# Block 0 of an adaLN transformer block on one core: keys due by chunk, the projection bank lent to row scores, modulation products and q/k parts on GpSimd, three pieces a projection

## The chip, the core and the metric

The kernel runs on one core of a Trainium2 chip. The core has five engines with instruction streams of their own: TensorE (PE, matrix multiplication into PSUM; its weight loads are shown as PEld), VectorE (DVE), ScalarE (ACT), GpSimd (POOL) and SyncE (SP), which here issues the DMAs. Each engine works through its stream in order; semaphores tie the streams together. The metric is the device time of one execution in microseconds, as the median over runs.

## The reference

One transformer block with adaptive layer norm: 2048 positions, width 576, 32 heads of 18, a feed-forward part of width 4608, all in float32.

```python
def _A_ref(x, wqkv, wo):                       # S = 2048, D = 576, H = 32
    qkv = (x @ wqkv).reshape(B, S, 3, H, D // H).transpose(2, 0, 3, 1, 4)
    q, k, v = qkv[0], qkv[1], qkv[2]
    p = softmax(einsum("bhqd,bhkd->bhqk", q, k) * Dh ** -0.5)
    return einsum("bhqk,bhkd->bhqd", p, v).transpose(0, 2, 1, 3).reshape(B, S, D) @ wo

def _B_ref(x, w1, w2):
    return silu(x @ w1) @ w2                   # F = 4608

mod = (silu(c) @ w_mod)                        # six vectors of 576: sa, ca, ga, sb, cb, gb
h = layernorm(x) * (1 + ca) + sa
x = x + ga * _A_ref(h, wqkv, wo)
h = layernorm(x) * (1 + cb) + sb
x = x + gb * _B_ref(h, w1, w2)
```

## The kernel before

**Precision.** Projections and feed-forward split each operand into a high part in the matmul type `float32r` and a low part (the rest), and add three products: high by high, high by low, low by high. So a q/k projection of 128 columns over 512 positions is 14 matmuls into one PSUM bank (list `PASS`), and its result is stored as a high and a low part (`qkhl`). The scores contract over three copies of the 18 head rows (54 rows), which is the same sum of products.

**Stages.** `first_part` normalizes x, transposes it to `hTh`/`hTl`, and computes v, the first two column tiles of k and, for the first 1024 positions, of q, and the first 80 row scores. Then the main loop goes over four blocks of 512 query positions (block 0 to 3) with eight quads of four heads each. Beside block 0 run the q/k projections still missing: 24 of them, `steps` and `add_qk`. Beside blocks 1 to 3 runs the output projection and feed-forward part (`post`) of the block before; that of block 3 runs alone at the end.

**A slot.** The loop counts slots; one `now` is half a slot: a matmul `psa` (line 802) of 128 queries by 512 keys, whose row maximum DVE takes (line 804), for a quad that is 40 slots ahead, and a matmul `psb` (line 852) of 128 keys by 512 queries of the current quad, whose exponential ACT takes (line 854, the tile `pt`). They use opposite row halves of PE, 64 rows each, and so run as a pair. A value step (line 889, `psv`) multiplies four `pt` tiles by v on four column strips of the array. A projection (line 591, `psqk`) uses all 128 rows. PSUM has eight banks; in block 0 three go to `psa` (pool `psA`), three to `psb`, one to the values, one to projections (`psF`).

**What sets the order.** PE's order is written out by the program itself: at each turn the main loop chooses between a score pair ("s"), value steps ("v") and the next item of a list of filler work ("f"). It does so by a clock of its own, `plan.t`, to which `plan.work` adds constants (ns): `TS` a score pair, `TV` a value step, `MMC` and `MMH` a matmul of 512 or 288 columns, `TX` for a change of the array's shape. DVE and ACT are two queues with durations (`plan.op`), and banks are rings: `plan.when("a")` says when the next bank of `psa` is free. The filler `Filler` is a list of small items, paced over the slots left; a projection stands in it as pieces of `GQ`. `fill.until` empties it up to a named item at once. The order on the other engines is not written by hand: the framework's scheduler places their instructions by a reckoning of its own.

**What block 0 fetches.** `load_quad` fetches a quad's q into SBUF and first asks with `need` for the projections of which that quad's k and q consist; `load_k` fetches a chunk of 512 keys. All go through SyncE's queue.

**The modulation products.** Of the six vectors of `mod`, two are computed in `first_part`; the other four come in block 0, 20 products in all (`cols`): `col_load` fetches a weight tile `wcl` of 128 by 576, and `col_dot` multiplies it by silu(c) (`sbc`) and sums the row, in one DVE instruction with an accumulator (line 514). The tile comes from the same ring of three buffers as `qkhl`.

**A projection's end.** The last piece of `qk_one` copies the bank twice on ACT, once as the high part (line 602) and once whole (`qt`, line 595); GpSimd subtracts (line 596); two DMAs store (lines 616 and 618).

## Time and profile before

| | |
|---|---|
| median of 3 runs | 2412.84 us (2409.73 to 2415.67) |
| profiled execution | 2407.57 us, span 2405.8 us |
| mean granted clock of PE | 0.992 |
| PE, DVE, ACT, POOL busy, of the span | 97%, 74%, 62%, 26% |
| first `psb` matmul of the main loop | 154.4 us |
| last projection matmul of block 0 | 530.4 us |
| first matmul of block 0's output projection | 577.1 us |
| last `psb` matmul | 2112.1 us |

The span is that of the profiled execution from its first to its last instruction. Engine rows give busy time; the time of an instruction on PE overlaps that of the next one, so starts tell more than busy shares there. A value matmul and a `psm` matmul are two records each in the trace, so a value step of four matmuls is eight records. In the groups, "idle before" is the engine's idle time ahead of the group's instructions, with what ended most of it.

### The profile page before, as it was taken

How to read it: one execution, taken by the hardware profiler on the slowest of the kernel's cores; microseconds unless marked ns; L12 is line 12 of the kernel's file. 1: busy time of each engine (PE TensorE's matmuls, PEld its weight loads, DVE VectorE, ACT ScalarE, POOL GpSimd, SP SyncE). 2: the span in 40 equal slices, each digit the busy share in tenths (PEclk: the TensorE clock that was granted, in tenths of full speed). 3: DMA queues.
4: the chain of work that ended last, by engine and by line, in shares of the span. 5: the costliest groups of instructions: out<-in, count | busy, mean ns of one | idle time of the engine just before them, and what ended most of it. 6: DMA issues, size and time to landing. Idle time of an engine off the chain costs nothing.

```text
span 2405.8 us, 52151 instructions
## 1 busy us (share of the span) xinstructions
PE 2323.4 (97%) x19844; PEld 1596.2 (66%) x19844; DVE 1775.2 (74%) x3109; ACT 1482.1 (62%) x2734; POOL 637.5 (26%) x769
## 2 busy tenths in 40 slices
PE   6999999998999999998999999999999999989999
PEld 4874444434567766775676777766677777678998
DVE  8768989887878888886887888887877787144333
ACT  5247777775667776675776777775676677722121
POOL 5201011104746676663311111122211111110000
PEclk9999999999999999999999999999999999999999
DMA  7555556445556666665655445554545554336563
GB/s 254 163 173 173 168 170 182 150 159 157 195 191 206 213 223 208 221 220 180 216 172 175 164 164 191 170 181 139 188 160 167 189 166 163 120 113 225 203 206 118
DMA packets 201474, 433.02 MB, mean 180 GB/s; under 512 B 31362, under 2 KB 67618, under 8 KB 201226
## 3 DMA queue, kind: packets, MB, share of 16 engines
q1 hardware_dynamic: 201226, 429.68, 54.5%
q8 instruction: 159, 2.61, 0.5%
q14 instruction: 89, 0.73, 0.1%
HBM read 338.54 MB, written 86.33 MB: 177 GB/s over the span
## 4 chain that ended last, share of the span: by engine, by line
PE 84%; DVE 7%; DMA 4%; ACT 3%; POOL 2%; issue 1%; SPq 0%; ACTq 0%; POOLq 0%; DVEq 0%
PE ps L486 25%; PE psv L889 18%; PE psa L802 13%; PE ps L480 10%; PE psb L852 8%; PE psqk L591 3%; DVE mx L804 3%; PE psp L486 2%; PE psv L486 2%; DMA raw<-in_w 1%; ACT pt L854 1%; PE psqk L486 1%; PE psv L1350 1%; PE psqk L1350 1%; PE psp L480 1%
## 5 line engine op out<-in xcount | busy, mean ns | idle before, releaser
L804 DVE TENSOR_REDUCE mx<-psa 128x1 f32<-128x512 f32 x2048 | 1319.0, 683 | 310.9 <-PE psb L852 161.8
L854 ACT ACTIVATE pt<-psb 128x512 f32<-128x512 f32 x2048 | 1131.5, 598 | 503.1 <-PE psb L852 305.8
L852 PE MATMUL psb<-qt,kb 56*128 56x512 f32 x2048 | 750.1, 423 | 10.7 <-ACT pt L854 9.7
L802 PE MATMUL psa<-ka,qt 54*128 54x512 f32 x2016 | 698.2, 415 | 9.5 <-DVE mx L804 8.0
L802 PEld LDWEIGHTS psa<-ka,qt 54*128 54x128 f32 x2016 | 335.2, 186 | 298.7 <-DVE mx L804 202.0
L889 PE MATMUL psv<-pt,vt 128*32 128x512 f32 x4096 | 513.5, 604 | 2.3 <-ACT ov L893 1.7
L486 PE MATMUL ps<-w2t,g 64*128 64x288 f32 x4992 | 410.5, 294 | 7.7 <-POOL w2t L693 3.9
L486 PEld LDWEIGHTS ps<-w2t,g 64*128 64x128 f32 x4992 | 382.7, 186 | 43.0 <-DVE mx L804 10.1
L852 PEld LDWEIGHTS psb<-qt,kb 56*128 56x128 f32 x2048 | 352.4, 185 | 53.6 <-ACT pt L854 38.4
L486 PE MATMUL ps<-hh,w1t 64*128 64x512 f32 x1944 | 371.6, 395 | 6.8 <-POOL w1t L696 3.1
L486 PEld LDWEIGHTS ps<-hh,w1t 64*128 64x128 f32 x1944 | 220.3, 186 | 44.9 <-DVE mx L804 7.5
L889 PEld LDWEIGHTS psv<-pt,vt 128*32 128x32 f32 x4096 | 99.5, 109 | 215.8 <-issue 208.0
L1125 POOL TENSOR_TENSOR g<-etmp,g 128x512 fp32r<-128x512 f32 x108 | 137.8, 1297 | 392.3 <-ACT g L1124 334.6
L1003 POOL TENSOR_TENSOR x<-x,gt 128x288 f32<-128x288 f32 x116 | 93.6, 807 | 416.9 <-ACT gt L1002 416.9
L486 PE MATMUL ps<-hl,w1t 64*128 64x512 f32 x864 | 198.0, 393 | 0.5 <-POOL hl L413 0.5
L999 DVE TENSOR_TENSOR x<-ps,x 128x288 f32<-128x288 f32 x184 | 83.8, 456 | 124.8 <-PE ps L480 77.1
L480 PE MATMUL ps<-w2t,g 128*128 128x288 f32 x960 | 133.5, 299 | 7.4 <-ACT g L1124 5.9
L480 PEld LDWEIGHTS ps<-w2t,g 128*128 128x128 f32 x960 | 131.1, 191 | 9.9 <-ACT g L1124 6.3
L486 PEld LDWEIGHTS ps<-hl,w1t 64*128 64x128 f32 x864 | 105.3, 186 | 10.8 <-POOL hl L413 0.9
L1121 ACT ACTIVATE eq<-ps 128x512 f32<-128x512 f32 x36 | 21.6, 600 | 146.3 <-PE ps L480 146.3
L480 PE MATMUL ps<-hh,w1t 128*128 128x512 f32 x360 | 106.9, 390 | 0.5 <-DVE hh L415 0.5
L1122 DVE SCALAR_TENSOR_TENSOR etmp<-etmp 128x512 f32<-128x512 f32 x108 | 76.6, 744 | 23.4 <-ACT etmp L1121 23.2
(146 smaller groups left out, 2084.4 us busy)
## 6 DMA issues: line engine op xcount, KB each, us to landing
w1t<-w1s SPq DMA_DIRECT2D x108, 640.0 KB
w2t<-w2s SPq DMA_DIRECT2D x108, 576.0 KB
kb<-kscr SPq DMA_DIRECT2D x512, 108.0 KB
ka<-kscr SPq DMA_DIRECT2D x504, 108.0 KB
w1s<-w1t SPq DMA_DIRECT2D x36, 640.0 KB
w2s<-w2t SPq DMA_DIRECT2D x36, 576.0 KB
vt<-vscr SPq DMA_DIRECT2D x32, 608.0 KB
qt<-qscr SPq DMA_DIRECT2D x128, 108.0 KB
```

Of the source, the lines that this page charges most:

```text
L480: mm(self.ps[late], lhsT=lhsT, rhs=rhs, start=(i == 0), stop=(i == self.n - 1))
L486: done = mm(self.ps[g], lhsT=lhsT[rows], rhs=rhs[rows], start=(s == 0), stop=(s == self.end))
L591: mm(qk_ps[0], lhsT=w[b][:, kt, :], rhs=(hTl if a else hTh)[:, kt, n * 512:(n + 1) * 512], start=(i == 0), stop=(i == 13))
L802: mm(ps, lhsT=t["q"][64 * j:64 * j + 54, hp, stt * P:(stt + 1) * P], rhs=t["a" if ("a", kc, hp) in t else "b", kc, hp][64 * j:64 * j + 54, ...
L804: return lambda: nc.vector.tensor_reduce(t["mx"][:, 2 * j + hp, stt, kc:kc + 1], ps, axis=AX.X, op=ALU.max)
L852: state["pe"] = mm(ps, lhsT=t["b", kt // 4, hp][64 * e:64 * e + 56, kt % 4 * P:(kt % 4 + 1) * P], rhs=t["q"][64 * e:64 * e + 56, hp, :], s ...
L854: nc.scalar.activation(t["P"][kt, hp][:, e, :], ps, AF.Exp, scale=SCALE)
L889: mm(t["ps"][32 * h:32 * h + 32, :], lhsT=t["v"][:, c0:c0 + 32], rhs=t["P"][kt, h // 2][:, h % 2, :], start=(kt == 0), stop=(kt == NKT - 1 ...
L999: nc.vector.tensor_add(c["x1"][j][:, hs], ps, c["x1"][j][:, hs])
L1003: nc.gpsimd.tensor_add(c["x1"][j][:, hs], c["x1"][j][:, hs], t)
L1122: nc.vector.scalar_tensor_tensor(t, t, 1.0, u, op0=ALU.add, op1=ALU.mult)
L1125: (nc.vector if last else nc.gpsimd).tensor_tensor(g[:, 1, :], t, f(g[:, 0, :]), op=ALU.subtract)
```

## The change

Seven edits, all but the constants in block 0:

1. A projection is cut in three pieces of 5, 5 and 4 matmuls, not in four of 4, 4, 3 and 3.
2. The planner's constants: `MMC`, `MMH`, `TS` and `TV` are lower, `TX` is higher, and a change to the full array costs two `TX`, not one. These hold in all blocks.
3. `col_dot` runs on GpSimd: a multiplication of 576 elements, then three halving additions (288, 144, 72); DVE sums the 72 left.
4. At a projection's end ACT copies the bank once; GpSimd makes the high part from that copy, then the low part. The bank is released after one ACT copy.
5. Each pair of column tiles computes q before k.
6. A quad's keys are asked for chunk by chunk, ahead of the load of each chunk, no longer all four with the quad.
7. If no bank of `psa` is free by the plan, a row score may take the projection bank when it is free.

```diff
--- before.py
+++ after.py
@@ -64,13 +64,13 @@
 GS = 2
 GR = [[range(i, min(i + GS, n)) for i in range(0, n, GS)] for n in (28, 27)]
 NG = len(GR[0])
-GQ = (range(0, 4), range(4, 8), range(8, 11), range(11, 14))
+GQ = (range(0, 5), range(5, 10), range(10, 14))
 G2 = [range(i, i + 3) for i in range(0, 24, 3)]
 GP = [range(i, i + 2) for i in range(0, 28, 2)]
-MMC = 231
-MMH = 133
-
-TS, TV, TX, TL, TR = 231, 906, 95, 430, 60
+MMC = 228
+MMH = 131
+
+TS, TV, TX, TL, TR = 229, 862, 112, 430, 60
 TMAX, TEXP = 605, 495
 TLAT = {"A": 100, "V": 85}
 AHEAD = 12
@@ -112,7 +112,7 @@
     def work(self, cost, mode="half"):
 
         if mode != self.mode:
-            cost += 2 * TX if mode == "half" else TX
+            cost += 2 * TX if mode in ("half", "full") else TX
             self.mode = mode
         self.t += cost
 
@@ -529,8 +529,16 @@
 
     def col_dot(m, t):
         w = col.pop((m, t))
-        after_pe(mod_dot(2 + m, t, w) if m < 2 else dot(w, gcol[:, m - 2, t:t + 1]))
-        plan.op("V", plan.t, 830)
+        dst = modc[:, 2 + m, t:t + 1] if m < 2 else gcol[:, m - 2, t:t + 1]
+        after_pe(nc.gpsimd.tensor_tensor(w, w, sbc, op=ALU.mult))
+        n = D
+        while n > 72:
+            n //= 2
+            nc.gpsimd.tensor_tensor(w[:, :n], w[:, :n], w[:, n:2 * n], op=ALU.add)
+        nc.vector.tensor_reduce(dst, w[:, :n], axis=AX.X, op=ALU.add)
+        if m == 1:
+            nc.vector.tensor_scalar_add(dst, dst, 1.0)
+        plan.op("V", plan.t + 6000, 160 if m == 1 else 80)
 
     def mod_load(m, t):
         dg = wqp.tile([P, P], F32, tag="dg", name="dg", bufs=1)
@@ -591,11 +599,12 @@
             mm(qk_ps[0], lhsT=w[b][:, kt, :], rhs=(hTl if a else hTh)[:, kt, n * 512:(n + 1) * 512], start=(i == 0), stop=(i == 13))
         if part == len(GQ) - 1:
 
-            hl, tmp = qk_hi(qk_ps[0]), qk_ps["t"].tile([P, 512], F32, name="qt")
+            hl, tmp = wqp.tile([P, 2, 512], F32R, tag="qk", name="qkhl", bufs=QKB), qk_ps["t"].tile([P, 512], F32, name="qt")
             nc.scalar.activation(tmp, qk_ps[0], AF.Copy)
+            nc.gpsimd.tensor_copy(hl[:, 0], tmp)
             nc.gpsimd.tensor_tensor(hl[:, 1], tmp, f(hl)[:, 0], op=ALU.subtract)
             qk_store(which, m, n, hl, (0, 1))
-            chain([("A", 600), ("A", 600)], plan.t + 200, None, qk_ps[1])
+            chain([("A", 600)], plan.t + 200, None, qk_ps[1])
 
     def qk_hi(ps):
         hl = wqp.tile([P, 2, 512], F32R, tag="qk", name="qkhl", bufs=QKB)
@@ -725,7 +734,7 @@
 
     steps = []
     for m in range(2, 4):
-        steps += [(KM, m, ((0, 1), (2, 3))), (QM, m, ((0, 1),))]
+        steps += [(QM, m, ((0, 1),)), (KM, m, ((0, 1), (2, 3)))]
     steps += [(XM, 0, ((0, 1), (2, 3)))]
     for m in range(4):
         steps += [(QM, m, ((2, 3),))]
@@ -748,9 +757,6 @@
     def load_quad(i):
         b, qd = divmod(i, NQUAD)
         t = quads.setdefault(i, {})
-        if b == 0:
-            for h in range(4 * qd, 4 * qd + 4):
-                need("k", h, 3)
         if b < NQB:
             for h in range(4 * qd, 4 * qd + 4):
                 need("q", h, b)
@@ -787,18 +793,22 @@
             load_quad(i + 1)
         n, w = divmod(s, 8)
         if w == 1:
+            i_, kc = divmod(n + 2, NKEY)
+            if i_ < NQUAD:
+                for h in range(4 * i_, 4 * i_ + 4):
+                    need("k", h, kc)
             if s == LEAD + 1:
                 load_k("a", n + 1, 0)
             load_k("a", n + 1, 1)
         elif w == 5:
             load_k("a", n + 2, 0)
 
-    def slot_mm(s, j):
+    def slot_mm(s, j, borrow=False):
         i, w = divmod(s, 32)
         kc, w = divmod(w, 8)
         hp, stt = divmod(w, 4)
         t = quads[i]
-        ps = psA.tile([P, 512], F32, tag="a", name="psa")
+        ps = psF.tile([P, 512], F32, tag="f", name="psa") if borrow else psA.tile([P, 512], F32, tag="a", name="psa")
         mm(ps, lhsT=t["q"][64 * j:64 * j + 54, hp, stt * P:(stt + 1) * P],
            rhs=t["a" if ("a", kc, hp) in t else "b", kc, hp][64 * j:64 * j + 54, :], start=True, stop=True)
         return lambda: nc.vector.tensor_reduce(t["mx"][:, 2 * j + hp, stt, kc:kc + 1], ps, axis=AX.X, op=ALU.max)
@@ -807,8 +817,9 @@
         if j == 0:
             slot_load(s)
         t = quads[s // 32]
-        slot_mm(s, j)()
-        plan.op("V", plan.t + TL - TS, TMAX, plan.take("a"))
+        borrow = not plan.is_ready(plan.when("a"))
+        slot_mm(s, j, borrow)()
+        plan.op("V", plan.t + TL - TS, TMAX, plan.take("f" if borrow else "a"))
         if j == 1 and s % 32 == 31:
             now = 2 * s + 1
             later.append((now, 0, 0, lambda: (max_a(t), max_rows(t)), None))
@@ -1554,6 +1565,9 @@
             fn()
             plan.advance()
 
+    def may_borrow():
+        return "p" not in mp and plan.is_ready(plan.when("f"))
+
     now = 2 * LEAD
     fill.pace(now, NQUAD * 64 - END0)
     stood = 0
@@ -1569,7 +1583,7 @@
         more = now < 2 * (total + LEAD)
         n = kts_ready()
         room = state["p"] + (now % 2 == 0) <= len(pts)
-        scores = more and room and plan.is_ready(plan.when("b")) and (now // 2 >= total or plan.is_ready(plan.when("a")))
+        scores = more and room and plan.is_ready(plan.when("b")) and (now // 2 >= total or plan.is_ready(plan.when("a")) or may_borrow())
         work = fill.pos < len(fill.items)
         target = fill.target() if work else now + AHEAD - 1
         ahead = now - target
```

PE, block 0, a stretch in the middle. Before, a piece of a projection (`psqk`), a run of three score pairs (`psa` and `psb` in turn) and a value step (`psv`):

```order
L591 MATMUL psqk<-hTl,wqh 128x512
L591 MATMUL psqk<-hTh,wqh 128x512
L591 MATMUL psqk<-hTh,wql 128x512
L802 MATMUL psa<-ka_82,qt 128x512
L852 MATMUL psb<-qt,kb_85 128x512
L802 MATMUL psa<-ka_82,qt 128x512
L852 MATMUL psb<-qt,kb_85 128x512
L802 MATMUL psa<-ka_83,qt 128x512
L852 MATMUL psb<-qt,kb_84 128x512
L889 MATMUL psv_3922<-pt_2036,vt_2040 32x512 x2
L889 MATMUL psv_3922<-pt_2037,vt_2040 32x512 x2
```

With the change, the last piece of a projection, a run of three pairs, a value step, and the first pair of the next run, which has three again (lines 599, 812, 863 and 900 of the change are 591, 802, 852 and 889 of before):

```order
L599 MATMUL psqk<-hTh,wql 128x512
L599 MATMUL psqk<-hTl,wqh 128x512
L599 MATMUL psqk<-hTh,wqh 128x512
L599 MATMUL psqk<-hTh,wql 128x512
L812 MATMUL psa<-ka_83,qt 128x512
L863 MATMUL psb<-qt,kb_85 128x512
L812 MATMUL psa<-ka_83,qt 128x512
L863 MATMUL psb<-qt,kb_85 128x512
L812 MATMUL psa<-ka_83,qt 128x512
L863 MATMUL psb<-qt,kb_84 128x512
L900 MATMUL psv_3981<-pt_2038,vt_2040 32x512 x2
L900 MATMUL psv_3981<-pt_2030,vt_2040 32x512 x2
```

The pieces are longer, and two pairs in a run have mostly become three. Over the whole stage from the first `psb` to the last `psqk` both orders have the same 473 score pairs, 117 value steps and 336 projection matmuls. Runs of score pairs: 194 before, 173 now; runs of full-array matmuls: 90 before, 68 now; runs of value steps: 117 in both. Sequences of three pairs, one value step and three pairs: none before, 41 now. All that stands ahead of the first `psb`, on each engine, is the same in both.

GpSimd, at the start of block 0's projections. Before, the subtraction at a projection's end (`qkhl`) and that of the next weights (`wql`):

```order
L596 TENSOR_TENSOR qkhl<-qt,qkhl 128x512 x3
L564 TENSOR_TENSOR wql<-raw,wqh 128x640
L596 TENSOR_TENSOR qkhl<-qt,qkhl 128x512 x2
L564 TENSOR_TENSOR wql<-raw,wqh 128x640
L596 TENSOR_TENSOR qkhl<-qt,qkhl 128x512 x4
L564 TENSOR_TENSOR wql<-raw,wqh 128x640
```

With the change, casts and subtractions (lines 604, 605) with the products of one modulation tile (`wcl`) among them:

```order
L604 CAST qkhl<-qt 128x512
L533 TENSOR_TENSOR wcl<-wcl,sbc 128x576
L605 TENSOR_TENSOR qkhl<-qt,qkhl 128x512
L537 TENSOR_TENSOR wcl<-wcl 128x288
L537 TENSOR_TENSOR wcl<-wcl 128x144
L537 TENSOR_TENSOR wcl<-wcl 128x72
L604 CAST qkhl<-qt 128x512
```

One instruction per projection has become two, and four more stand there per modulation tile, here with the first of them between the two of a projection.

DVE, at the first modulation product. Before, the product itself stands among the row maxima (`mx`):

```order
L804 TENSOR_REDUCE mx<-psa 128x1 x38
L514 SCALAR_TENSOR_TENSOR wcl,gcol<-wcl,sbc 128x576
L537 TENSOR_SCALAR dg<-ident,gcol 128x128
L804 TENSOR_REDUCE mx<-psa 128x1 x20
L514 SCALAR_TENSOR_TENSOR wcl,gcol<-wcl,sbc 128x576
L804 TENSOR_REDUCE mx<-psa 128x1 x7
```

With the change, the reduction of what GpSimd leaves:

```order
L814 TENSOR_REDUCE mx<-psa 128x1 x45
L538 TENSOR_REDUCE gcol<-wcl 128x1
L545 TENSOR_SCALAR dg<-ident,gcol 128x128
L814 TENSOR_REDUCE mx<-psa 128x1 x19
L829 TENSOR_REDUCE negm<-mx 128x16
L832 CAST ms<-negm 128x2x8
```

The product has left DVE's stream, the short reduction stands some rows later in it. The bank of projections is lent to one of the 472 row scores in this stage in the built program.

## The prediction

> **What bounds the kernel now.** I read the page first (busy shares, the chain that ended last), then busy time by stage, then the stage of the change one PE instruction at a time.
>
> ```profile
> span 2405.8 us, 52151 instructions
> PE 2323.4 (97%) x19844; PEld 1596.2 (66%) x19844; DVE 1775.2 (74%) x3109; ACT 1482.1 (62%) x2734; POOL 637.5 (26%) x769
> PE 84%; DVE 7%; DMA 4%; ACT 3%; POOL 2%; issue 1%; SPq 0%; ACTq 0%; POOLq 0%; DVEq 0%
> ```
>
> PE carries 84% of the chain, DVE 7%. The change sits in block 0, from the first `psb` matmul to the last projection matmul:
>
> ```profile
> L852 PE MATMUL psb<-qt,kb x2048: 386/397/625, 154.4 to 2112.1; 56*128 56x512 f32 x187
> L591 PE MATMUL psqk<-hTh,wql x120: 387/396/504, 155.6 to 530.4; 128*128 128x512 f32 x120
> 154.40:530.40 376.00, 371.65 (x2241) 157.46 (x2238) 329.84 (x584) 281.10 (x545) 40.39 (x32) 1.00 0.53 165
> 530.40:577.00 46.60, 42.91 (x238) 16.53 (x239) 38.41 (x67) 34.45 (x64) 24.15 (x34) 1.00 0.69 210
> 1200.00:1600.00 400.00, 399.54 (x3972) 289.79 (x3969) 324.38 (x542) 285.48 (x526) 65.23 (x63) 1.00 0.51 170
> ```
>
> In those 376.0 us (columns: PE, weight loads, DVE, ACT, POOL) PE is called busy for 371.65, DVE for 329.84, POOL for 40.39. Yet PE starts only 2241 instructions, 6.0 per us, against 9.9 from 1200 to 1600. So the busy share hides something, and the starts show what:
>
> ```profile
> 300.52 0.49 PE L802 MATMUL psa<-ka,qt 54*128 54x512 f32 x1
> ...
> 301.43 0.50 PE L591 MATMUL psqk<-hTl,wqh 128*128 128x512 f32 x1
> ...
> 305.72 1.06 PE L889 MATMUL psv<-pt,vt 128*32 128x512 f32 x8
> 306.72 0.49 PE L802 MATMUL psa<-ka,qt 54*128 54x512 f32 x1
> ...
> 307.38 0.50 PE L591 MATMUL psqk<-hTh,wqh 128*128 128x512 f32 x1
> 307.71 0.39 PE L591 MATMUL psqk<-hTh,wql 128*128 128x512 f32 x1
> ...
> 309.10 0.39 PE L591 MATMUL psqk<-hTh,wql 128*128 128x512 f32 x1
> 309.42 0.50 PE L802 MATMUL psa<-ka,qt 54*128 54x512 f32 x1
> 799.62 1.86 PE psv L889 x16
> 721.19 2.71 PE psv L889 x24
> ```
>
> PE runs in three shapes of the array: score pairs on row halves (`psa`, `psb`), projections on all of it (`psqk`), value steps on column strips (`psv`). Inside a run of projections starts follow by (309.10 - 307.71) / 6 = 0.23 us. The run of eight takes 309.42 - 307.38 = 2.04 = 8 x 0.23 + 0.20. The run of three pairs takes 0.91, that of two 0.66: 0.23 a pair and about 0.21 for the run. A value step (eight records) takes 1.00, two in the chain 1.86, three 2.71: 0.86 a step and 0.14 a run. So **each change of shape costs 0.14 to 0.21 us**, and a sum of steps and runs can be held against the stage:
>
> ```profile
> L852 PE MATMUL psb<-qt,kb 56*128 56x512 f32 x473 | 168.6, 442 | 2.3 <-ACT pt L854 1.7
> L889 PE MATMUL psv<-pt,vt 128*32 128x512 f32 x936 | 124.7, 604 | 0.6 <-DMA vt<-vscr 0.6
> ```
>
> 473 pairs x 0.23 = 108.8; 936 / 8 = 117 value steps x 0.857 = 100.3; 24 projections of 14 x 0.23 = 77.3; ten small `psm` about 1. Work: 287.4. The built order of before has 194 score runs, 90 projection runs and 117 value runs here: 40.7 + 18.0 + 16.4 = 75.1. Together 362.5 of 376.0: **PE waits for only some 13.5 us**, and loses 75 to changes of shape.
>
> **The change part by part.** *Runs.* With three pieces a projection and with the new planner costs, the order of the change has, for the same instructions in this stage, 173 score runs, 68 projection runs and 117 value runs. That is 21 x 0.21 + 22 x 0.20 = **8.8 us less**, directly on the path. Behind the last projection the order is the same up to the output projection of block 0. From there on only the planner's constants act: 224 score runs become 218, 219 value runs 213, 6 full-array runs 7: 1.3 + 0.8 - 0.2 = **1.9 us less**.
>
> *Products on GpSimd.* The costs:
>
> ```profile
> L804 DVE TENSOR_REDUCE mx<-psa 128x1 f32<-128x512 f32 x468 | 295.9, 682 | 45.0 <-PE psb L852 32.7 <-PE psa L802 10.4
> L514 DVE SCALAR_TENSOR_TENSOR wcl<-wcl,sbc 128x576 f32<-128x576 f32 x20 | 15.4, 769 | 0.0
> L514 DVE DVE_READ_ACCUMULATOR wcl<-wcl,sbc 128x1 f32 x20 | 1.6, 81 | 0.0
> L818 DVE TENSOR_REDUCE negm<-mx 128x16 f32<-128x64 f32 x7 | 1.5, 213 | 0.1
> L596 POOL TENSOR_TENSOR qkhl<-qt,qkhl 128x512 fp32r<-128x512 f32 x23 | 29.7, 1290 | 214.8 <-ACT qt L595 92.9 <-DVE mx L804 64.3 <-DMA kb<-kscr 29.3
> L1003 POOL TENSOR_TENSOR x<-x,gt 128x288 f32<-128x288 f32 x116 | 93.6, 807 | 416.9 <-ACT gt L1002 416.9
> L602 ACT ACTIVATE qkhl<-psqk 128x512 fp32r<-128x512 f32 x24 | 14.5, 606 | 3.6 <-PE psqk L591 3.5
> L693 POOL CAST wo<-raw x10: 417/426/466, 545.3 to 570.4; 128x288 fp32r<-128x288 f32 x10
> ```
>
> DVE loses 15.4 + 1.6 = 17.0 us and gains 20 reduces of 72 elements; the nearest row is the one of 64 elements, 0.21 us, so 4.2. Net 12.8 us free of 329.84. GpSimd gains per product 576 elements (1290 x 576 / 512 = 1.45 us), 288 (0.81), 144 and 72 (0.41 and 0.20 in proportion): 2.9 us, 20 times 58. *q/k parts.* ACT loses 24 x 0.606 = 14.5 us; GpSimd gains 24 casts of 0.426 x 512 / 288 = 0.76 each, 18. POOL goes from 40.4 to about 117 of 367 us, so it has room, and a part comes 0.76 us later to its store.
>
> None of this is PE's own work; it can take from the 13.5 us of waits, or add. The earlier release of the projection bank (one ACT copy, not two) helps in the same way. Bounds: all of them gone, -13.5; for the upper end see the rivals. I take 0, since two things pull against each other. For less waiting: DVE and ACT are 13 and 14 us freer. For more: in 41 places three pairs, one value step and three pairs now follow directly, which before has nowhere in this stage. Such a cycle is 0.21 + 0.69 + 1.00 = 1.90 us of PE, and three row maxes take
>
> ```profile
> 304.51 1.89 DVE L804 TENSOR_REDUCE mx<-psa 128x1 f32<-128x512 f32 x3 [0.37 <-PE psa L802]
> 542.19 2.48 DVE L804 TENSOR_REDUCE mx<-psa 128x1 f32<-128x512 f32 x4 [0.65 <-PE psb L852]
> 541.65 0.50 PE L802 MATMUL psa<-ka,qt 54*128 54x512 f32 x1
> ...
> 544.79 0.50 PE L802 MATMUL psa<-ka,qt 54*128 54x512 f32 x1
> ```
>
> 1.89, or 3 x 0.62 by the run of four. There is no margin, so DVE's other work in these 78 us becomes wait. That other work is 329.84 less 473 maxes at 0.63 (295.9 / 468), 31 us, less 17.0 and with 4.2: 18 us over the stage, of which 78 / 367 is 4 us. Against that stand some 4 us of the relief.
>
> *Keys by chunk.* It moves when K is due, and adds no instruction. What it removes is small:
>
> ```profile
> SPq L761 <- DMA qscr<-qkhl: 4.6, 2, 3.9
> SPq L618 <- POOL qkhl L596: 8.4, 12, 1.4
> ```
>
> Twice the queue of loads stands up to 3.9 us for a q part just stored, and key loads are queued behind it. In the new order the shortest way from a store to its load is several score runs long. Keys are fetched eight slots (sixteen scores) ahead, so I count nothing; if that cover is gone, 4.6 us. *The lent bank.* In the built program it serves 1 of the stage's row scores: nothing.
>
> Sum: -8.8 - 1.9 + 0 = **-10.7 us**: span 2395.1, that run 2396.9 for 2407.57. The median shown, 2412.84, lies 5.3 above the profiled run, so 2402.
>
> **The rivals.** *A, the waits take it back.* Each of the 41 tight cycles waits longer than its share. The row from 541.65 to 544.79 is such a case: 3.14 us for 0.21 + 0.92 + 1.00 = 2.13 of work, 1.0 lost a cycle; 41 of them would be 41 us. Against that full price: there PE stood for exponentials with two `psb` banks, and this stage has three. At 0.15 to 0.35 each, 6 to 14 us: 2408 to 2416, no change by measure.
>
> *B, slower: the reduce stands in DVE's queue.* DVE runs in order, so a reduce whose GpSimd chain isn't done holds all row maxes behind it, and these hold the score banks. The chain takes 2.9 us, 4.2 where a q/k subtraction stands inside it. For it: the SyncE row above, where the planned order trusted GpSimd too early in 12 places, by up to 1.4 us. Three banks cover about one max, 0.6; at 1.4 late 20 x 0.8 = 16 us, at 2.0 late 28. From about 1.1 us late on average it decides: 2402 + 16 to 28, 2418 to 2430. Against it: DVE's order is not written by hand; the scheduler puts the reduce where, by its own reckoning, the chain is done.
>
> ```profile
> L911 DVE TENSOR_TENSOR ou<-ou,rec x32: 440/459/1554, 213.6 to 2119.0; 128x288 f32<-128x288 f32 x32
> ```
>
> A second price in B is collision: this DVE multiply, whose inputs both lie in SBUF, once took 1554 ns for 459; its seven in the stage could lose 7.7 us. The Trainium skill (SBUF — State Buffer, "SBUF: two separate sides") says that GpSimd and such a DVE instruction take one port pair in turn, and that the later one stands until the other's instruction ends; by it GpSimd's work would speak against the change, at those 7.7 us, and I give this 0.03 of B's chance. It leaves the row maxes out, whose input is not in SBUF.
>
> *C, more: the waits go as well.* The freed DVE and ACT take 10 of the 13.5 us: 2392. For it: DVE is busy 88% of the stage and PE stood for both engines; against: the same tight cycles.
>
> **How the numbers follow.** The forecast (-6 to -16: 2397 to 2407) 0.48, A 0.27, B 0.14, C 0.11. A measurement of this kernel tells 0.3%, 7.2 us, from nothing. The forecast's part beyond that is about 0.41; with C, faster 0.52. A and the forecast's rest: same 0.33. Slower: B and a tip of A, 0.15. The order of the later blocks also meets their own stalls anew:
>
> ```profile
> 577.00:700.00 123.00, 108.75 (x922) 70.51 (x922) 89.09 (x168) 69.38 (x127) 67.91 (x93) 0.94 0.52 171
> 1100.00:1200.00 100.00, 91.41 (x881) 63.00 (x883) 75.67 (x148) 60.27 (x110) 33.04 (x39) 0.97 0.57 190
> ```
>
> PE idles 14 and 9 us there at a granted clock of 0.94 and 0.97; half of one more or less is 5 to 7 us. Low end: C's 2392 less 2. High end: past A, up to B's lower end, 2419. This leaves out most of B and a little of C.
>
> **What would show it.** Right: the last projection near 520 to 524 us, the rest of the kernel's length within some 6 us of before's, runs costing what they cost now, DVE some 13 us and ACT some 14 us less busy in the stage, POOL some 77 more. For A: a gap before the third `psa` of a run of three, ended by a row max. For B: idle DVE before the new reduces, ended by GpSimd. The forecast is wrong if a run's price depends on what is waited for inside it, or if the later blocks' stalls move by more than 8 us.

## The result, and the profile after

The change takes 2378.82 us (median of 4 runs, 2376.31 to 2381.41) against 2414.26 for the kernel before (4 runs): ratio 0.9857, interval 0.9845 to 0.987. That is 35 us less; 2402 was predicted, with a low end of 2390. The direction was right, the size was not. First the page of the change (span; engine rows; chain by engine):

```profile
span 2375.7 us, 52168 instructions
PE 2306.1 (97%) x19844; PEld 1576.7 (66%) x19844; DVE 1784.3 (75%) x3089; ACT 1479.9 (62%) x2710; POOL 714.1 (30%) x873
PE 85%; DVE 6%; DMA 3%; POOL 2%; ACT 2%; issue 1%; SPq 0%; DVEq 0%; POOLq 0%; ACTq 0%
```

The span is 30.1 us shorter. The other 5 us of the medians' difference can't be placed: the profiled execution of before lies 6.7 us below its median, that of the change 1.3. These three rows say nothing of why: but for POOL (30% for 26%), busy shares are within a point of before's. So the span is cut at four marks that every version has: first `psb`, last `psqk`, first matmul of block 0's output projection (`psp`), and the 769th `psb`, the middle of block 1. Busy time by stage, first of before, then of the change (PE, weight loads, DVE, ACT, POOL, granted clock, DMA share, GB/s):

```profile
577.09:2401.97 1824.88, 1778.74 (x16232) 1308.30 (x16228) 1294.67 (x2235) 1113.49 (x2035) 527.68 (x650) 0.99 0.55 181
832.85:2401.97 1569.12, 1537.45 (x14014) 1142.64 (x14011) 1096.65 (x1889) 948.48 (x1734) 375.71 (x443) 0.99 0.54 179
```

```profile
154.40:519.30 364.90, 361.53 (x2241) 158.24 (x2238) 322.21 (x563) 269.07 (x522) 115.69 (x135) 1.00 0.54 170
519.30:566.10 46.80, 43.01 (x240) 16.35 (x240) 38.92 (x67) 34.10 (x64) 24.75 (x35) 1.00 0.69 218
566.06:2371.91 1805.85, 1771.47 (x16231) 1288.27 (x16228) 1310.95 (x2235) 1123.71 (x2035) 528.64 (x651) 0.99 0.55 182
566.06:818.77 252.71, 240.75 (x2222) 163.23 (x2218) 200.61 (x346) 165.45 (x301) 155.47 (x211) 0.97 0.59 193
818.77:2371.91 1553.14, 1530.72 (x14013) 1125.05 (x14010) 1110.34 (x1889) 958.26 (x1734) 373.17 (x441) 0.99 0.54 181
```

The projection stage went from 376.0 to 364.9 (-11.1), the tail of block 0 stayed at 46.6 to 46.8, the first half of block 1 became 255.8 - 252.7 = 3.1 shorter, and **all behind it became 16.0 shorter**, with the same work on PE (14014 and 14013 starts) and no edit there but the planner's constants. By the prediction's own sum (work, plus 0.21 a score run, 0.20 a full-array run and 0.14 a value run; the rest is waiting), with the runs counted in the traces (194, 90 and 117 before; 172, 67 and 117 now), waits in the projection stage went from 13.5 to 11.6 us. From `psp` to the end they went from some 113 to 96, while changes of shape there went from 73.7 to 71.8; the 113 is an estimate, with 0.132 us for a pair of matmuls of 288 columns, the median there, but the 17.1 between the two doesn't depend on it.

The 17 us don't lie in one wait. The first half of block 1 has 3.4 of them. The rest, divided into five pieces of 256 `psb` matmuls and what follows the last of these, has 2.4 to 3.9 us less waiting in five of the six and 2.0 more in one. The piece that shortens most, by 7.7 us of which 3.5 are waiting, before and then with the change:

```profile
1602.50:1867.00 264.50, 259.24 (x2488) 177.56 (x2486) 211.50 (x376) 179.21 (x332) 53.03 (x55) 0.99 0.53 173
1585.80:1842.62 256.82, 252.69 (x2474) 176.31 (x2472) 213.68 (x374) 181.25 (x330) 52.18 (x54) 1.00 0.55 178
```

Block 0's engines, in the groups of the changed page's trace, projection stage (busy, mean ns | idle before and what ended it):

```profile
L812 PEld LDWEIGHTS psa<-ka,qt 54*128 54x128 f32 x473 | 75.6, 185 | 125.6 <-DVE mx L814 103.0 <-issue 8.4 <-DVE mt L835 1.7
L533 POOL TENSOR_TENSOR wcl<-wcl,sbc 128x576 f32<-128x576 f32 x20 | 28.5, 1426 | 43.7 <-PE psb L863 38.8 <-DMA ou<-ov 2.2 <-PE psa L812 2.0
L537 POOL TENSOR_TENSOR wcl<-wcl 128x288 f32<-128x288 f32 x20 | 16.1, 804 | 1.3
L537 POOL TENSOR_TENSOR wcl<-wcl 128x144 f32<-128x144 f32 x20 | 10.1, 504 | 1.6
L537 POOL TENSOR_TENSOR wcl<-wcl 128x72 f32<-128x72 f32 x20 | 7.0, 352 | 1.6
L604 POOL CAST qkhl<-qt 128x512 fp32r<-128x512 f32 x23 | 14.0, 610 | 128.9 <-ACT qt L603 114.8 <-DMA kscr<-qkhl 9.6 <-DVE rec L921 4.5
L538 DVE TENSOR_REDUCE gcol<-wcl 128x1 f32<-128x72 f32 x10 | 2.2, 217 | 0.6 <-POOL wcl L537 0.6
L538 DVE TENSOR_REDUCE modc<-wcl 128x1 f32<-128x72 f32 x10 | 2.2, 216 | 0.0
L922 DVE TENSOR_TENSOR ou<-ou,rec 128x288 f32<-128x288 f32 x7 | 4.2, 602 | 0.2
```

A product costs GpSimd 1.43 + 0.80 + 0.50 + 0.35 = 3.09 us (2.9 predicted), a cast 0.61 (0.76). GpSimd has 115.7 us of work instead of 40.4, and the next engine hardly sees it: before the new reduces DVE stood 0.6 us in all. The first row above, the weight loads of `psa`, is to be held against before's, whose wait for row maxima (`mx`) is a little shorter:

```profile
L802 PEld LDWEIGHTS psa<-ka,qt 54*128 54x128 f32 x473 | 74.9, 185 | 127.3 <-DVE mx L804 99.4 <-issue 12.0 <-ACT pt L854 2.5
```

### The profile page after: what moved, and what is told of

Same layout as the page of the kernel before. It is cut to its first block, busy times and chain, and to the rows that moved or that the text cites. A ratio compares the mean times of both kernels' runs of the same rounds, so it can differ in the third digit from the quotient of the medians.

```text
span 2375.7 us, 52168 instructions
## 1 busy us (share of the span) xinstructions
PE 2306.1 (97%) x19844; PEld 1576.7 (66%) x19844; DVE 1784.3 (75%) x3089; ACT 1479.9 (62%) x2710; POOL 714.1 (30%) x873
## 4 chain that ended last, share of the span: by engine, by line
PE 85%; DVE 6%; DMA 3%; POOL 2%; ACT 2%; issue 1%; SPq 0%; DVEq 0%; POOLq 0%; ACTq 0%
PE ps L486 25%; PE psv L900 18%; PE psa L812 14%; PE ps L480 10%; PE psb L863 8%; PE psqk L599 4%; DVE mx L814 2%; PE psv L486 2%; PE psp L486 1%; DMA raw<-in_w 1%; PE psqk L486 1%; PE psv L1361 1%; ACT pt L865 1%; PE psqk L1361 1%; PE psp L480 1%
## 5 line engine op out<-in xcount | busy, mean ns | idle before, releaser
L865 ACT ACTIVATE pt<-psb 128x512 f32<-128x512 f32 x2048 | 1143.0, 598 | 482.6 <-PE psb L863 294.0
L812 PE MATMUL psa<-ka,qt 54*128 54x512 f32 x2016 | 722.8, 416 | 9.2 <-DVE mx L814 8.0
L486 PE MATMUL ps<-hh,w1t 64*128 64x512 f32 x1944 | 359.9, 395 | 5.2 <-POOL w1t L704 1.8
L486 PEld LDWEIGHTS ps<-hh,w1t 64*128 64x128 f32 x1944 | 197.8, 187 | 50.6 <-DVE mx L814 5.9
L486 PE MATMUL ps<-hl,w1t 64*128 64x512 f32 x864 | 180.9, 393 | 0.0
L486 PEld LDWEIGHTS ps<-hl,w1t 64*128 64x128 f32 x864 | 90.2, 187 | 15.3
```

Of the source, the lines that this page charges most:

```text
L486: done = mm(self.ps[g], lhsT=lhsT[rows], rhs=rhs[rows], start=(s == 0), stop=(s == self.end))
L812: mm(ps, lhsT=t["q"][64 * j:64 * j + 54, hp, stt * P:(stt + 1) * P], rhs=t["a" if ("a", kc, hp) in t else "b", kc, hp][64 * j:64 * j + 54, ...
L865: nc.scalar.activation(t["P"][kt, hp][:, e, :], ps, AF.Exp, scale=SCALE)
```

## The experiments

Eighteen kernels, each read by the same marks. "Block 0" is the first `psb` to the first `psp`, "1a" runs from there to the 769th `psb`, "1b on" to the last matmul. The three lengths are those of one profiled execution. The ratio is to executions of before taken beside each kernel, whose medians run from 2410.3 to 2414.3 us.

| kernel | median us | ratio to before, interval | block 0 | 1a | 1b on |
|---|---|---|---|---|---|
| before | 2414.26 | | 422.6 | 255.8 | 1569.1 |
| the change | 2378.82 | 0.9857 (0.9845 to 0.987) | 411.7 | 252.7 | 1553.1 |
| e1_const_only | 2397.21 | 0.993 (0.9918 to 0.9942) | 419.3 | 258.9 | 1556.6 |
| e2_no_const | 2406.17 | 0.9969 (0.9958 to 0.998) | 428.7 | 249.0 | 1569.0 |
| e3_const_block0 | 2398.76 | 0.9936 (0.9922 to 0.9951) | 414.2 | 254.9 | 1569.0 |
| e4_const_late | 2398.56 | 0.9943 (0.993 to 0.9956) | 424.9 | 257.7 | 1552.7 |
| l1_late_tv | 2398.71 | 0.9949 (0.9931 to 0.9966) | 414.2 | 252.7 | 1568.8 |
| l2_late_mm | 2383.79 | 0.9879 (0.9864 to 0.9893) | 411.9 | 250.6 | 1564.0 |
| l3_late_over | 2392.88 | 0.9914 (0.9899 to 0.9928) | 411.7 | 253.4 | 1562.9 |
| l4_late_near | 2379.82 | 0.9862 (0.9847 to 0.9877) | 411.5 | 252.4 | 1553.3 |
| p1_old_plus4 | 2392.07 | 0.992 (0.9898 to 0.9942) | 412.4 | 258.8 | 1554.9 |
| p2_new_plus4 | 2386.2 | 0.9897 (0.9876 to 0.9917) | 413.2 | 250.6 | 1556.1 |
| p3_old_minus6 | 2409.78 | 0.9996 (0.9987 to 1.0006) | 412.3 | 257.5 | 1577.8 |
| p4_new_minus6 | 2405.51 | 0.9983 (0.9973 to 0.9993) | 414.4 | 252.1 | 1575.4 |
| p_keep5_old | 2400.72 | 0.9943 (0.9926 to 0.996) | 414.5 | 254.6 | 1572.2 |
| p_keep5_new | 2395.2 | 0.9921 (0.9906 to 0.9936) | 412.8 | 254.4 | 1564.8 |
| b0_four | 2390.81 | 0.9904 (0.9887 to 0.9922) | 414.4 | 258.2 | 1553.3 |
| b0_engines | 2390.97 | 0.9908 (0.9886 to 0.993) | 423.2 | 251.3 | 1557.5 |
| b0_dots | 2383.69 | 0.9888 (0.9873 to 0.9903) | 416.5 | 250.8 | 1554.7 |
| b0_keys | 2385.81 | 0.9902 (0.9885 to 0.9919) | 411.9 | 259.6 | 1553.0 |

### Constants, block 0, or both

e1 is the kernel before with edit 2 alone, e2 the change without it. In e3 and e4 the constants switch where block 0's work ends, by a dictionary:

```diff
+TF = 2
+COST0 = dict(MMC=228, MMH=131, TS=229, TV=862, TX=112, TF=2)
+COST1 = dict(MMC=231, MMH=133, TS=231, TV=906, TX=95, TF=1)
...
-            cost += 2 * TX if mode in ("half", "full") else TX
+            cost += 2 * TX if mode == "half" else TF * TX if mode == "full" else TX
...
+    globals().update(COST0)
...
     def open_mlp():
         nonlocal psF, psA, psX
+        globals().update(COST1)
```

This is e3, the change with the old constants in the later blocks; e4 is the kernel before with the two sets the other way round.

> Before with the planner's new constants alone, in all blocks. Theory 1 (the constants make the later blocks wait less): the stretch behind the last projection shrinks by 17 to 21 us as with the change, and the projection stage by 2 to 4 us for its 2.4 us fewer changes of shape: 20 to 25 us less than before in all. Theory 2 (the later blocks gain from what block 0's edits on engines and keys do): 2 to 6 us less in all. Theory 3 (any new order of the later blocks falls anywhere within some 10 us): no fixed size.

> The change with the planner's old constants, so all other edits remain. Theory 1: the projection stage is 8 to 11 us shorter (8.5 us of changes of shape are saved in its order), the later stretch as before within 3 us: 8 to 14 us less in all. Theory 2: nearly all of the 35 us remains, 28 or more. Theory 3: projection stage as in theory 1, the rest anywhere within 10 us.

> The change, with the old constants put back when the projections end, so that the later blocks are ordered as before and block 0 as with the change. Theory 1: 11 us less than before in all, the stretch behind the last projection within 3 us of before's. Theory 2: 28 us less or more. Theory 3: like theory 1, since the later order is before's.

> Before, with the new constants only from the end of the projections on: block 0 as before, later blocks ordered as with the change. Theory 1: 18 to 24 us less than before, all of it behind the last projection; with the kernel that has them in block 0 alone it adds up to the change's 35. Theory 2: within 4 us of before. Theory 3: like theory 1, since the later order is the change's; orders by other constants have to tell the two apart.

The stretch "1b on" settles where the 16 us come from: 1569 wherever the later blocks have the old constants (before, e2, e3), 1553 to 1557 with the new ones (the change, e1, e4), whatever block 0 has. Here e2 and then e4:

```profile
833.55:2402.55 1569.00, 1538.04 (x14014) 1142.57 (x14011) 1099.17 (x1889) 947.90 (x1734) 376.62 (x442) 0.99 0.54 179
839.67:2392.39 1552.72, 1529.88 (x14014) 1121.26 (x14010) 1109.67 (x1889) 958.26 (x1734) 374.96 (x441) 0.99 0.54 181
```

Theory 2, a gain handed down by block 0's edits, falls. Theory 1's sizes were not met either: the medians of e1 and e4 are 17 and 16 us lower, for 20 to 25 and 18 to 24, with 1a longer in both (258.9 and 257.7), and e2 misses "as before within 3" (from `psp` on it is 7 us shorter, all of it in 1a). An order mostly repeats closely. The three with before's later order lie within 0.2 us of each other; the seven with the change's (the change, e1, e4 and the four b0 versions) run from 1552.7 to 1557.5. Block 0's gain also needs the constants: with the edits and the old constants (e2) it takes 428.7 us, 6 more than before. Its projection stage is short there too (365.4), but its order leaves more value runs behind the last projection, and that tail takes 63.3 for 46.8.

### Which constant, and is it the better fit?

Four versions of the `COST1` of e3: only `TV`; only `MMC`, `MMH` and `TS`; all moved by as much as in the change, but the other way; and a set a little beyond the new one.

```diff
-COST1 = dict(MMC=231, MMH=133, TS=231, TV=906, TX=95, TF=1)
+COST1 = dict(MMC=231, MMH=133, TS=231, TV=862, TX=95, TF=1)
...
+COST1 = dict(MMC=228, MMH=131, TS=229, TV=906, TX=95, TF=1)
...
+COST1 = dict(MMC=234, MMH=135, TS=233, TV=950, TX=78, TF=1)
...
+COST1 = dict(MMC=227, MMH=130, TS=228, TV=857, TX=115, TF=2)
```

> The change, with only the cost of a value step new in the later blocks (862); the other costs there are the old ones, block 0 is as with the change. From the first matmul of block 0's output projection to the end the change takes 1810, the change with old costs there 1828. Theory 1 (a cost near the measured one lets PE wait less): the value step was the cost furthest off (906 for 0.857 measured), so this takes most of the gain: 1812 to 1820. Theory 3 (a new order falls anywhere): 1808 to 1838.

> The change, with only the costs of score pairs and of matmuls of 512 and 288 columns new in the later blocks (229, 228, 131). Theory 1: these were off by 1 to 2%, but carry most of PE's time: 1816 to 1824 from the first matmul of the output projection to the end. Theory 3: 1808 to 1838.

> The change, with the costs of the later blocks moved the other way, beyond the old ones: value step 950, score pair 233, matmuls 234 and 135, change of shape 78. Theory 1: PE runs further ahead of the planner's clock and waits more: 1832 to 1850 from the first matmul of the output projection to the end. Theory 3: 1808 to 1838, as likely below the old costs' 1828 as above.

> The change, with costs in the later blocks that lie beside the new ones (value step 857, score pair 228, matmuls 227 and 130, change of shape 115), so that the order is another one but the planner's clock nearly the same. Theory 1: within 5 us of the change's 1810 from the first matmul of the output projection to the end. Theory 3: 1808 to 1838.

The value step's cost, which moved most (906 to 862), gives nothing in "1b on": 1568.8. Three constants that move by 2 to 3 ns each give 5. The other direction (l3) gives 6. In the window of the expectations, to the end of the program, l1, l2, l3 and l4 take 1825, 1818, 1820 and 1810 us: l1 and l3 miss Theory 1's ranges, l2 lies in its range. So the size of the correction doesn't order the results, which speaks against Theory 1, waits that shrink because the planner's clock is truer. l4 says nothing on it: its order turned out to be nearly that of the change (188 of 212 value runs at the same place).

### The same constants at another place

Three pairs shift the order by a number that isn't a cost, from block 1 on, once with the old constants and once with the new: `END`, the half-slot at which the filler is to be through (from -4 to 4, and to -10), and `KEEP`, a limit of the main loop (from 6 to 5).

```diff
-COST1 = dict(MMC=231, MMH=133, TS=231, TV=906, TX=95, TF=1)
+COST1 = dict(MMC=231, MMH=133, TS=231, TV=906, TX=95, TF=1, END=4)
...
+COST1 = dict(MMC=231, MMH=133, TS=231, TV=906, TX=95, TF=1, END=-10)
...
+COST1 = dict(MMC=231, MMH=133, TS=231, TV=906, TX=95, TF=1, KEEP=5)
```

> The change with the old costs in the later blocks, and the later blocks' filler paced to end 8 half slots later (END 4 for -4), which shuffles their order: less than a quarter of the value runs stand where they stood. It is the partner of the next run, with the same pacing and the new costs. Theory 1 (the costs): this one is 12 to 20 us longer behind block 0 than its partner. Theory 3 (each order falls where it falls): old and new costs differ by anything from -10 to +10 us.

> The change itself (new costs everywhere) with the same shifted pacing. Theory 1: 12 to 20 us shorter behind block 0 than its partner with old costs, and within 8 us of the change. Theory 3: anywhere within 10 us of its partner, and up to 20 us above the change, whose order was then a lucky one.

> As the first of these four, with the pacing shifted the other way (END -10 for -4), old costs in the later blocks. Theory 1: 12 to 20 us longer behind block 0 than its partner. Theory 3: within 10 us of it, with either sign.

> The change itself with the pacing shifted the other way. Theory 1: 12 to 20 us shorter behind block 0 than its partner with old costs, within 8 us of the change. Theory 3: within 10 us of its partner, up to 20 us above the change.

> The same lowered limit with the old constants from open_mlp on; 200 of 220 value runs stand where they stood before. Both theories: 1a to the end near 1824 us (within 4), the kernel near 2398; it is the partner of the run above. Theory C puts 12 to 18 us between the two, theory L 4 to 8.

> The change, with one limit of the main loop lowered from open_mlp on (KEEP from 6 to 5), which leaves the new constants but brings an order near to the one before in the later blocks (138 of 222 value runs at the same place). Theory C (the constants give the later blocks' gain whatever the order): 1a to the end takes 1806 to 1812 us, the kernel about 2379 to 2386. Theory L (the order's place gives most of it, the constants some 4 to 8 us): 1814 to 1820 us, the kernel 2388 to 2394. Projection stage and tail as in the change.

The stretch "1b on" by stage windows, p1, p2, p3 and p4 in turn:

```profile
825.15:2380.02 1554.87, 1537.45 (x14013) 1141.94 (x14011) 1099.22 (x1890) 948.74 (x1734) 375.00 (x441) 0.99 0.54 180
```

```profile
819.75:2375.81 1556.06, 1534.20 (x14006) 1120.05 (x14002) 1104.84 (x1889) 958.53 (x1734) 373.33 (x439) 0.99 0.54 180
```

```profile
824.00:2401.80 1577.80, 1544.41 (x14020) 1146.50 (x14019) 1095.38 (x1889) 946.40 (x1734) 377.67 (x444) 0.99 0.53 178
```

```profile
822.39:2397.74 1575.35, 1539.44 (x14022) 1130.35 (x14018) 1109.55 (x1888) 957.56 (x1734) 377.77 (x443) 0.99 0.53 178
```

With the *old* constants, `END` alone reaches 1554.9, 14 of the change's 16 us; with the *new* ones, `END` loses them all: 1575.4. New against old at the same place is +1.2, -2.4, -7.4 and, in the change against e3, -15.8; the first two are no more than one order varies. So the later gain belongs to the order at which the planner arrives, and a few nanoseconds in a cost are one way of many to arrive at another. The whole spread of "1b on" over all versions is 1553 to 1578, and the change sits at its lower edge. Read over everything from `psp` on, the three pairs say 7.1, 7.8 and 7.5 us for the new constants, as theory L had it, and not the 12 to 20 of Theories 1 and C. Most of the first two lies in 1a, whose length is another matter (below). Still, the new constants are shorter in all four pairs (by 18.0 in the change against e3), so that some microseconds may be theirs on average; four pairs don't settle it.

### 1a, and block 0's edits one at a time

Each of these undoes one thing of the change and keeps the rest; from the last projection on their orders have all but one or two of the change's value runs at the same place.

```diff
-GQ = (range(0, 5), range(5, 10), range(10, 14))
+GQ = (range(0, 4), range(4, 8), range(8, 11), range(11, 14))
```

b0_four is this. b0_dots puts the modulation products back:

```diff
+        after_pe(mod_dot(2 + m, t, w) if m < 2 else dot(w, gcol[:, m - 2, t:t + 1]))
+        plan.op("V", plan.t, 830)
```

b0_engines does that and gives ScalarE its second copy again (edit 4 undone); b0_keys undoes edits 5 and 6.

> The change with four pieces a projection (4, 4, 3, 3) again. Block 0's projection stage then has 188 score runs, 89 projection runs and 118 value runs, for 173, 68 and 117 of the change: 15 x 0.205 + 21 x 0.20 + 0.14 = 7.4 us more by the price of a change of shape. Theory P (the pieces give the stage's gain): the stage takes 364.9 + 7.4 = 372 us, the kernel about 2386. Theory E (the freed VectorE and ScalarE, or the other edits of block 0, give it): the stage stays within 2 us of 364.9 and the kernel near 2379. The later blocks have the change's order and should take its 1805.9 us within 3.

> The change with the modulation products in one VectorE instruction each and the high part of q and k on ScalarE again; three pieces, keys by chunk and the constants stay. Runs in the projection stage: 178 score, 72 projection, 112 value: 5 x 0.205 + 4 x 0.20 - 5 x 0.14 = 1.1 us more. Theory P: 366 us for the stage, 2380 for the kernel, since what GpSimd takes over lies beside PE's work. Theory E: VectorE, 13 us fuller, and ScalarE, 14 us fuller, make PE wait: 370 us or more, 2384 or more.

> The change with the modulation products in one VectorE instruction each again; all else stays. Its projection stage has 166 score, 66 projection and 113 value runs for 173, 68 and 117 of the change (2.4 us less of changes of shape, and 4 value steps, 4 us, moved behind the last projection). Stage and tail together take 411.7 us in the change and 423.1 with both engine moves undone. Theory V (VectorE's 13 us are what is saved): 420 us or more here, the kernel near 2388. Theory A (ScalarE's 14 us and the bank released after one copy save it): 411 to 415, the kernel near 2380. In equal parts: about 417.

> The change with all four key chunks asked for with the quad and K ahead of Q again; all else stays. Runs in the stage: 172, 68 and 117, as in the change but for one. The prediction counts nothing for this edit: stage and tail 411.7 within 2 us, the kernel 2379 within 4. The rival prices the loads that stand behind a store just made: up to 4.6 us more, 2384, with waits of the queue of loads for qscr as long as before (2 of 2.3 us on average) or longer.

The windows of block 0 (projection stage, tail) in b0_four, b0_engines and b0_dots:

```profile
154.01:525.43 371.42, 368.51 (x2260) 156.28 (x2256) 324.46 (x568) 272.96 (x526) 114.95 (x135) 1.00 0.54 168
525.43:568.45 43.02, 39.38 (x221) 14.85 (x221) 36.04 (x62) 31.48 (x59) 23.30 (x33) 1.00 0.70 226
```

```profile
157.08:522.92 365.84, 362.96 (x2192) 159.62 (x2188) 321.47 (x571) 273.68 (x532) 40.46 (x32) 0.99 0.54 167
522.92:580.23 57.31, 52.19 (x288) 20.12 (x288) 47.56 (x79) 41.20 (x76) 24.89 (x35) 1.00 0.67 206
```

```profile
153.99:514.48 360.49, 356.62 (x2193) 156.93 (x2190) 323.69 (x572) 262.80 (x510) 54.41 (x55) 1.00 0.54 170
514.48:570.50 56.02, 51.67 (x286) 19.70 (x286) 46.42 (x77) 40.10 (x74) 27.50 (x39) 1.00 0.67 216
```

The lesson is to read both windows. Four pieces make the stage 371.4, as theory P had it (372), but the tail 43.0, since fewer starts are left for it (221 for 240): 414.4 together, no more than the 411.5 to 414.5 that the change's own block 0 takes in the eleven versions that keep it (e3, all l and p). By the sum, waits are 4.4 us less than in the change (22.4 for 26.8 over both windows) and changes of shape 7.1 more: long runs pay in waits a good part of what they save in changes. b0_engines keeps its stage at 365.8, again as theory P had it, and takes 10.5 more in the tail: 423.2 together, 11.5 more, of which 8.9 is waiting. The products alone are 4.8 of that, near the 417 of "in equal parts"; the rest would be the copy on ScalarE, which wasn't undone alone. b0_keys stands at 411.9: the keys give nothing in block 0, as predicted.

So **block 0 is shorter with the work moved to GpSimd**, as theory E had it, but by how much depends on the order around it. With four pieces and new constants it is 4.8 us (b0_four against e1, 414.4 for 419.3, edits 5 to 7 among them), with three pieces 11.5, and with the old constants (e2) block 0 is 6 us longer than before in spite of it, with 15 us more waiting than in the change. To undo a move also changes what the planner counts for VectorE and ScalarE, and with it the order: the tails of b0_engines, b0_dots and e2 all hold 18 value steps, the change's holds 15. Whether the freed engines or the order that comes with them make the difference, these runs don't separate.

b0_four's median lies 12 us above the change's, though, and its windows hold 2.7 in block 0 and 5.5 in 1a: the profiled execution was the fastest of its four, so some 4 us of it aren't placed. b0_engines' 12 us in the median are about those of block 0; its profiled execution, 4 us above its median, has 4.3 us more in "1b on" as well.

b0_keys is 7 us slower as a whole, all of it in 1a (259.6 for 252.7). PE's waits for 645 to 662 us, the change and then b0_keys (total, times, longest):

```profile
PE ps L486 <- POOL w1t L704: 1.8, 1, 1.8
PE ps L486 <- POOL w1t L705: 1.7, 1, 1.7
```

```profile
PE ps L486 <- POOL w1t L704: 6.1, 2, 3.4
PE ps L486 <- POOL w1t L705: 3.2, 1, 3.2
```

The first feed-forward matmuls stand for their weights, which GpSimd casts after a load; in b0_keys its chain is this, with products of another kind (`g`) ahead:

```profile
647.56 0.76 POOL w2t L705
648.32 1.75 POOL g L1135
...
653.58 4.50 DMA raw<-in_w
658.08 0.05 issue
658.14 0.45 POOL w1t L704
```

1a takes 249.0 to 259.6 us over the table, with old and new constants alike (old: 249.0 to 258.8, new: 250.6 to 259.6). The seven versions with the change's later order alone take 250.8 to 259.6. It isn't settled what moves this arrival from one version to the next; 3 of the change's 35 us are of this kind.

## Why the prediction was right or wrong

**Right: the price of a change of shape and the run counts.** In the changed kernel's stage a run of three pairs still takes 0.91 us, five projection matmuls 1.36 and a value step 1.00 (medians, from a run's start to the next one's), and the counts came within one. The stage went down by 11.1 for 8.8. But b0_four shows that "directly on the path" was wrong: it has 7.1 us more in changes of shape, and block 0 as a whole is 2.7 longer, no more than one order varies. What longer runs save comes back in good part as waits.

**Right by luck: "I take 0" for block 0's waits.** The stage's waits fell by 1.9 only, but undoing one edit moves them by more: block 0 waits 8.9 us longer with the moves undone, 4.4 less with four pieces, 15 more with the old constants. That they cancel in this order is nothing that the prediction's two parts of some 4 us could tell.

**Right: what each engine gains and loses.** POOL +75.3 for +77; ACT -12.0 for -14.5; DVE's instructions, added one by one, -10.5 for -12.8: 17.0 gone, 4.3 of new reduces, and 2.1 in two groups that grew longer (below). Its busy time, which counts overlapping records once, fell by 7.6.

**Right: keys nothing in block 0; the lent bank is open.** The keys were undone alone; the bank, lent once in 472, was not.

**Wrong, and this is the error: the later blocks.** "From there on only the planner's constants act" was right, and then only their runs were priced, 1.9 us. The waits there were some 113 us, eight times those of the stage over which the prediction argued at length, and the order changes in all of them: only about a quarter of some 213 value runs keep their place. The prediction saw it ("meets their own stalls anew") and priced it at "half of one more or less", 5 to 7 us, and took nothing of it into the sum. Measured: 17.1 us less waiting. Its own sign of being wrong, later stalls that move by more than 8 us, came. That they moved down was the draw of this order: the pairs above reach 1578 as well as 1553, and the range needed these 25 us by which orders of the same work differ.

**The rivals.** A didn't come: waits in the stage fell, and the wait of `psa` for row maxima rose by 3.6 us (99.4 to 103.0), the size that the prediction gave tight cycles, not the 6 to 14 of A. B didn't come: 0.6 us of DVE before the reduces. Its second price, the collision with GpSimd, would be 2 us, not 7.7. The seven multiplies take 4.2 us, for 4.3 in the same stage before, but two smaller groups are longer, with before's rows first (min, median and max ns, then the mean in the stage):

```profile
L537 DVE TENSOR_SCALAR dg<-ident,gcol x10: 240/280/288, 174.3 to 450.0; 128x128 f32<-128x128 f32 x10
L822 DVE TENSOR_TENSOR ms<-negm,ms 128x16 fp32r<-128x16 f32 x7 | 2.3, 323 | 0.1
```

```profile
L545 DVE TENSOR_SCALAR dg<-ident,gcol x10: 274/320/576, 177.7 to 419.2; 128x128 f32<-128x128 f32 x10
L833 DVE TENSOR_TENSOR ms<-negm,ms 128x16 fp32r<-128x16 f32 x7 | 3.3, 473 | 0.2
```

The ten `dg` take 3.8 us for 2.7, the seven `ms` 3.3 for 2.3. The `dg` follow GpSimd's work: on average they take 273 to 281 ns in the four versions that leave products and casts to DVE and ACT (before, e1, e4, b0_engines), 304 with the casts alone on GpSimd (b0_dots), and 358 to 449 in all others. The mean of `ms` varies more: 168 to 324 in those four, 339 to 532 with both on GpSimd. Their inputs lie in SBUF, and the row maxima, whose input doesn't, kept their 682 to 683 ns. That agrees in kind with the Trainium skill's rule of the port pair taken in turn (SBUF — State Buffer, "SBUF: two separate sides"); that it is this rule, no run here shows. C came in part, 1.9 us of the 10 that it asked for in the stage.

## What to carry to other kernels

Where a planner writes the order, any number it reads, a cost moved by 2 ns or an end moved by a few slots, can draw another order for all that follows; here orders of equal work lie up to 25 us apart. Price such an edit by the waits of every stage it reaches, not by the stage it was made for, and try several neighbours before crediting the number itself. When an edit moves work across a mark, add the windows on both sides before reading a gain.

## What the runs showed of the hardware

GpSimd's short adds don't shrink in proportion to their length: by the profile 288, 144 and 72 elements take 804, 504 and 352 ns, 2.1 ns an element and some 0.2 us for each instruction (worked out from the first and the last), so a halving chain costs more in its short end than proportion says. The Trainium skill (GPSIMD Engine Reference, "Elementwise — side-by-side cycle accounting") has some 2.6 cycles at 1.2 GHz an element for such an addition, an estimate of 2.2 ns by that page, and the trace agrees; for the 0.2 us it has no figure. A cast of 512 elements into `fp32r` takes 610 ns there, under half of a subtraction with the same result (1286 ns in the group of line 605), so the high part was the cheap one to move. And one order repeats rather closely: three versions with before's later order gave 1569.1, 1569.0 and 1569.0 us, seven with the change's 1552.7 to 1557.5. So a difference of more than some 5 us in this stretch is more than the repeats of one order show; a smaller one may not be the order's.
